# An attention and feed-forward kernel: all attention products in plain float32, eight first-stage weight chunks instead of six

## The chip, the cores and the metric

The kernel runs on one NeuronCore of a Trainium2 chip. The metric is the device time of one execution in microseconds (us). TensorE (PE) multiplies matrices; VectorE (DVE), ScalarE (ACT) and GpSimd (POOL) work on elements; SyncE (SP) issues the transfers between the large memory (HBM) and the on-chip memory. TensorE writes its results into eight PSUM banks of 128 x 512 float32 values, from which DVE or ACT copies them. Each engine runs its own list of instructions in order, and waits where an instruction needs another engine's result.

## The reference

```python
scores = q @ k.T / 8                       # B=4, H=8 heads, S=576 rows, D=64; causal mask
a = exp(scores - rowmax); a /= a.sum() + 1e-9
local = a @ v
q_p = where(q > 0, q, exp(q) - 1) + 1
mem_out = (q_p @ M_prev) / (q_p @ z_prev + 1e-6)
x = sigmoid(beta) * mem_out + (1 - sigmoid(beta)) * local   # -> (2304, 512)
h = x @ w_in                                # (2304, 2048)
g = (a0 + a1 h + a2 h^2 + a3 h^3) / (1 + |b0||h| + |b1| h^2 + 1e-6)
out = g @ w_out                             # (2304, 512)
```

The results are float32. `w_in` and `w_out` come as 64-bit floats, which the kernel turns into 32-bit ones itself.

## The kernel before

The attention is done in 16 units of work: 4 batches times 4 pairs of heads, `u` from 0 to 15. For a unit, `load` brings q, k and v of two heads, `prep` transposes q and k on TensorE (line L505) and makes the transposed, normalized `q_p` (tile `E`, then `f`). `scores` makes q.k for four 128-row tiles of each head (128, 256, 384 and 512 columns wide) and `tail` for the last 64 rows of both heads together. `prob` then makes the softmax of each: DVE adds the mask and takes the maximum (L706), ACT the exponential and its sum (L710), POOL or DVE the reciprocal's input (L718, L719), DVE the reciprocal (L721), and POOL, ACT or DVE scales the rows (L722 to L724). TensorE transposes the probabilities, they are copied to tiles `g0` and `g1`, and `av` multiplies them by v and adds the memory's part; its result, `x`, is written to the scratch tensor `xs` in HBM (`spill`).

TensorE is used in two number formats. Plain float32 (F32) is run as two passes over the columns for each product. The reduced format F32R is run as one, and keeps fewer digits; to get them back, an operand is split in two F32R parts, a rounded one (`hi`) and the rest (`lo`), and three products are made in place of one. `hi_lo` (L536 ff.) does the split out of PSUM: a copy on ACT or DVE (L541, L542), and a subtraction on DVE (L547), or on TensorE and ACT (L494 with `nid`, L545). Before the change all scores are made so: the split, transposed q and k (tile `tt`) are moved by transfers into the tiles `qk0` and `qk1`, in which the parts of one head stand under each other, so that two products per tile of rows do. For the products with v the first five units (`PLAIN`) use plain float32 (tiles `gp`, `vz`, `mz`, `fp`), the other eleven the split form (`g`, `vs`, `ms`, `f`, `fl`, and `s`, by which the two halves of a result are added).

The feed-forward part works on groups of 256 rows (9 of them) and on 16 chunks of 128 hidden columns. Its weights are converted to 32 bits and split (`weights`: four DVE instructions, two of POOL and one of ACT for each half of a chunk). The first `F0` = 6 chunks are kept from early on (tile `w`); the first stage runs all groups through them, from `xs`, and writes partial sums to `po`. The other ten (tiles `w2i`, `w2o`) use memory that the attention leaves at its end; the second stage runs all groups through them. For two chunks of a group TensorE makes 24 products of 256 columns (`bk<-xg,w`) and 12 of 512 (`bk<-w,gh` and `bk<-w,gl`), with a chain of element-wise work on DVE, ACT and POOL between them (`act_chain`).

The order of all instructions is set when the kernel is built: `Sched.place` takes, again and again, the operation that could start first by its own table of costs, ties broken by priority; buffers and PSUM banks are given out by `Tag.can` and `Tag.take`. On the chip the order of each engine's list is fixed, and only the waits decide when an instruction starts. The attention of unit `u` has priority 100 u and what follows, so it goes ahead of the feed-forward work, which fills what is free.

Of the kernel before, what the change touches and what calls it, by code (L numbers as in the profile page):

```python
# [25 lines left out]
SLOT = 150  # L26
# [64 lines left out]
class Tag:  # L91
# [8 lines left out]
    def can(self, seq):  # L100

        return len(self.free) > (0 if seq == self.head else 1)
# [15 lines left out]
class Sched:  # L118
# [64 lines left out]
    def place(self):  # L183
# [64 lines left out]
        while pend:  # L248
            best = None
            for o in pend:  # L250
                slot_t = 0.0
                ok = True
                for b in o.bufs:
                    if b.slot is None:
                        tg = b.tag
                        if not tg.can(b.seq) or b.kind and not b.kind.can(b.kseq):
                            ok = False
                            break
                        slot_t = max(slot_t, min(tg.free)[0] + SLOT)
# [57 lines left out]
def tile_attention_ffn(  # L317
# [105 lines left out]
    for n in ("qk0", "qk1"):
        for x in tags(atp, n, N[n], [128, 3, SM], F32R):
            for j in range(4):
                V.tensor_scalar(x[64:128, 2, 128 * j:128 * j + 128], idf[64:128, :], 0.0, None, op0=ALU.mult)

    tags(atp, "tt", N["tt"], [128, 4 * SM + 128], F32R)

    for x in tags(atp, "qd", N["qd"], [128, 2, 128], F32R):  # L430
        for i in range(2):
            r = slice(64 * i, 64 * i + 64)
            V.tensor_scalar(x[r, :, 64 - 64 * i:128 - 64 * i], idf[r, :].rearrange("p (a b) -> p a b", a=2), 0.0, None, op0=ALU.mult)
    tags(atp, "f", N["f"], [128, 2, S], F32R)
    tags(atp, "fl", N["fl"], [128, S], F32R)
    tags(atp, "vs", N["vs"], [128, 5, 4, 64], F32R)
    tags(atp, "ms", N["ms"], [128, KC, 4, 64], F32R)
    tags(atp, "mn", N["mn"], [128, KC, 2, 64])
# [6 lines left out]
    tags(atp, "g0", N["g0"], [128, 2, 384], F32R)  # L445
    tags(atp, "x", N["x"], [128, S])
    tags(atp, "s", N["s"], [128, 320], F32R)

    plx = ExitStack()
    if PLAIN:
        plp = plx.enter_context(tc.tile_pool(name="plp", bufs=1))
        tags(plp, "gp0", 1, [128, 2, 384])
        tags(plp, "gp1", 1, [128, 2, 4, 320])
        tags(plp, "fp", 1, [128, S])
        for n, shape in (("vz", [128, 5, 2, 128]), ("mz", [128, KC, 128])):
            for x in tags(plp, n, 1, shape):
                G.memset(x, 0.0)  # L460
    for i in range(2):
        sc.tag(f"g1{i}", 1).free = []
# [787 lines left out]
```

## Time and profile before

| | |
|---|---|
| median of 3 runs | 723.14 us (720.86 to 726.55) |
| profiled execution, first to last instruction | 722.8 us; no other time of it is given |
| attention (last write of `xs` issued) | 365 us |
| first stage's last product with `w_out` | about 456 us |
| TensorE's granted clock, mean | 0.974 of 2.4 GHz |

The page of the profile shows how long each engine was busy; TensorE's spans are modelled and overlap, so that a busy share near one is not yet its peak. How long a product really takes is read from the starts of instructions that follow each other without a gap.

### The profile page before, as it was taken

The numbers are of one execution on the slowest core, as the hardware profiler recorded it, in microseconds if no ns is written. First come the engines' busy times: TensorE is split into PE (matmuls) and PEld (weight loads), VectorE is DVE, ScalarE is ACT, GpSimd is POOL, SyncE is SP. The second block draws the span as 40 slices with busy tenths as digits, with TensorE's granted clock in tenths as the row PEclk, the third lists the DMA queues.
The fourth block names the chain that finished last, engine by engine and source line by source line (L and its number), as shares of the span: only waits on it lengthen the run. The fifth ranks groups of instructions, "written<-read, shape, count | busy, mean of one in ns | idle before, by whom it ended". The sixth has DMA issues, their size and how long they took to land.

```text
span 722.8 us, 12139 instructions
## 1 busy us (share of the span) xinstructions
PE 659.6 (91%) x3752; PEld 561.2 (78%) x3752; DVE 588.3 (81%) x1385; ACT 480.6 (66%) x1072; POOL 492.7 (68%) x599
## 2 busy tenths in 40 slices
PE   3879798799898999799999999886999999999997
PEld 2667576687777778688899998775998888788786
DVE  5787697799998999689877999989786776866775
ACT  2767576789888798769666766474575552851852
POOL 4476666678877679636568999769775663763763
PEclk9999989899999999899999999998999999999999
DMA  6877888685788774944267543721580103003001
GB/s 139 204 198 180 205 197 195 153 227 122 212 220 211 173 171 123 257 115 106 98 211 244 171 155 125 258 63 58 185 311 31 58 1 116 1 1 114 4 0 59
DMA packets 102577, 102.51 MB, mean 142 GB/s; under 512 B 67632, under 2 KB 80432, under 8 KB 100208
## 3 DMA queue, kind: packets, MB, share of 16 engines
q1 hardware_dynamic: 102512, 101.73, 50.4%
q8 instruction: 30, 0.49, 0.3%
q14 instruction: 35, 0.29, 0.1%
HBM read 52.27 MB, written 23.59 MB: 105 GB/s over the span
## 4 chain that ended last, share of the span: by engine, by line
PE 40%; DVE 22%; POOL 11%; ACT 9%; DMA 8%; issue 6%; SPq 3%; POOLq 0%; ACTq 0%; DVEq 0%
PE bk L494 37%; POOL tw L521 4%; PE bk L505 4%; DVE bk L706 3%; SPq L487 3%; DVE tb L1026 2%; DVE g L547 2%; DVE gh L527 1%; POOL tw L1021 1%; DVE bk L527 1%; ACT g L541 1%; DVE bk L1028 1%; DVE gl L1041 1%; ACT Ps L710 1%; DMA xf<-xs 1%
## 5 line engine op out<-in xcount | busy, mean ns | idle before, releaser
L494 PE MATMUL bk<-w2o,gh 128*128 128x512 f32 x360 | 111.1, 390 | 0.9 <-DVE gh L527 0.9
L521 POOL TENSOR_TENSOR tw<-tw,gh 128x512 f32<-128x512 f32 x60 | 77.8, 1301 | 33.2 <-DVE gh L527 33.0
L1021 POOL TENSOR_SCALAR tw<-ta,cb 128x512 f32<-128x512 f32 x71 | 57.4, 808 | 62.8 <-ACT ta L1017 62.4
L521 POOL TENSOR_TENSOR tw<-tw,ta 128x512 f32<-128x512 f32 x72 | 94.2, 1309 | 3.8
L1017 ACT ACTIVATE ta<-bk 128x512 f32<-128x512 f32 x72 | 42.8, 595 | 71.8 <-PE bk L494 53.6
L494 PE MATMUL bk<-w,w2i 128*128 128x512 f32 x360 | 84.9, 390 | 0.0
L494 PE MATMUL bk<-xg,w 128*128 128x256 f32 x648 | 83.5, 284 | 0.0
L494 PEld LDWEIGHTS bk<-xg,w 128*128 128x128 f32 x648 | 80.5, 191 | 2.8 <-ACT x L898 0.8
L706 DVE CUSTOM_DVE_ANT_0 bk<-bk,mk 128x512 f32<-128x512 f32 (+3 forms) x144 | 72.4, 519 | 11.7 <-PE bk L494 11.0
L494 PEld LDWEIGHTS bk<-w,w2i 128*128 128x128 f32 x360 | 67.3, 188 | 14.6 <-DVE gl L1041 0.5
L494 PE MATMUL bk<-w2o,gl 128*128 128x512 f32 x180 | 70.8, 393 | 8.6 <-DVE gl L1041 8.6
L1025 ACT ACTIVATE ta<-tw,lnb 128x512 f32<-128x512 f32 x72 | 52.0, 723 | 39.7 <-POOL tw L521 39.3
L494 PEld LDWEIGHTS bk<-w2o,gh 128*128 128x128 f32 x360 | 66.9, 188 | 14.6 <-DVE gh L527 1.3
L494 PE MATMUL bk<-qk 128*128 128x256 f32 (+3 forms) x256 | 67.4, 364 | 7.7 <-DMA qk<-tt 4.9
L527 DVE SCALAR_TENSOR_TENSOR bk<-bk,ca,tw 128x512 f32<-128x512 f32 x72 | 54.2, 753 | 21.9 <-POOL tw L521 21.6
L494 PE MATMUL bk<-w,gh 128*128 128x512 f32 x216 | 69.7, 404 | 0.0
L718 POOL TENSOR_SCALAR st<-st,g 128x1 f32<-128x1 f32 x88 | 26.5, 301 | 56.5 <-ACT Ps L710 47.1
L1026 DVE TENSOR_TENSOR tb<-bk,tb 128x512 f32<-128x512 f32 x72 | 49.3, 685 | 15.8 <-ACT tb L1018 12.6
L1028 DVE SCALAR_TENSOR_TENSOR bk<-tb,ca,bk 128x512 f32<-128x512 f32 x72 | 54.0, 750 | 9.1 <-ACT ta L1017 8.3
L527 DVE SCALAR_TENSOR_TENSOR gh<-bk,ca,ta 128x512 fp32r<-128x512 f32 x72 | 53.5, 743 | 8.1 <-PE bk L494 4.3
L547 DVE TENSOR_TENSOR g<-bk,g 128x512 fp32r<-128x512 f32 (+2 forms) x88 | 49.6, 567 | 8.7 <-ACT g L541 7.6
L710 ACT ACTIVATE Ps<-bk,st 128x128 f32<-128x128 f32 (+1 forms) x96 | 46.0, 482 | 11.5 <-DVE st L721 5.5
(151 smaller groups left out, 1702.0 us busy)
## 6 DMA issues: line engine op xcount, KB each, us to landing
qk<-tt SPq DMA_DIRECT2D x32, 384.0 KB, 4.7
xh<-xg SPq DMA_DIRECT2D x9, 1024.0 KB, 4.9
qk<-tt SPq DMA_DIRECT2D x32, 256.0 KB, 4.0
xf<-in_moe_w_in_dram SPq DMA_DIRECT2D x16, 512.0 KB, 4.7
xf<-in_moe_w_out_dram SPq DMA_DIRECT2D x16, 512.0 KB, 4.6
w<-xh SPq DMA_DIRECT2D x6, 1024.0 KB, 9.1
xs<-x SPq DMA_DIRECT2D x16, 288.0 KB, 2.3
xf<-xs SPq DMA_DIRECT2D x9, 512.0 KB, 5.8
```

The lines of the kernel that those rows point to most:

```text
L494: T.matmul(o, lhsT=l, rhs=r, start=s0, stop=s1, skip_group_check=more)
L505: T.matmul(o, lhsT=i, rhs=idn, start=x == 0, stop=True, is_transpose=True, skip_group_check=x > 0)
L521: opts = {"pool": ("pool", c_pool2(n), lambda: G.tensor_tensor(**kw()), "t"), "dve": ("dve", c_dve(n), lambda: V.tensor_tensor(**kw()), "2")}
L527: return dve(c_dve(n) + 61 * ap, lambda: V.scalar_tensor_tensor(out=out(), in0=in0(), scalar=scalar() if callable(scalar) else scalar, in1 ...
L547: dve(c_dve(n), lambda: V.tensor_tensor(out=lo(), in0=src(), in1=rb(hi()), op=ALU.subtract), [rsrc] + whi, wlo, pri)
L706: V.tensor_tensor_reduce(out=s, in0=s, in1=m, scale=-0.125, scalar=st.t[:, 0:1] if x else 3.0e38, op0=ALU.add, op1=ALU.min, accum_out=st.t ...
L710: act(c_act(w, ap=2), lambda bk=bk, w=w, x=x, c0=c0: A.activation(P.t[:, c0:c0 + w], bk.t[:, 0:w], AF.Exp, bias=st.t[:, mx:mx + 1], scale= ...
L1017: act(c_act(N), lambda: A.activation(a_(), h(), AF.Abs), [(hb, None)], [(ta, None)], p)
L1021: sc.op([("pool", c_pool(N, 2), lambda: G.tensor_scalar(w_(), a_(), cb[:, 1:2], cb[:, 0:1], op0=ALU.mult, op1=ALU.add), "s"), ("act", c_ac ...
L1025: act(c_act(N, False, 1), lambda: A.activation(a_(), w_(), AF.Ln, scale=2.0 ** -63, bias=lnb[:, 0:1]), [(tw, None)], [(ta, None)], p)
L1026: dve(c_dve(N), lambda: V.tensor_tensor(out=b_(), in0=h(), in1=b_(), op=ALU.mult), [(hb, None)], [(tb, None)], p)
L1028: dve(c_dve(N) + 61, lambda: V.scalar_tensor_tensor(out=h(), in0=b_(), scalar=ca[:, 1:2], in1=h(), op0=ALU.add, op1=ALU.mult), [(tb, None) ...
```

## The change

Every product of the attention is made in plain float32. `hi_lo`, the split tiles, the transfers `qk<-tt` and `f<-fl`, and the sum of halves (`s`, `fold`) are gone; a transposed q and k lie in one tile, `kt`, as they come out of PSUM, head 0 in partitions 0 to 63 and head 1 in 64 to 127. `scores` makes both heads' products one after the other, each on its own 64 partitions (64 rows of TensorE's array) and into its own bank. `av` makes one result for both heads: head 0 goes to partitions 0 to 63 of the bank, head 1 to 64 to 127, each with v as 64 columns of weights. Most attention tiles have two buffers instead of one (`nq`, `nk`, `kt`, `qd`, `g1`, `x`, ...), and `Tag.can` is asked for all of an operation's buffers at once. `FIRST` is 8 instead of 6, so the first stage has eight chunks and the second eight.

```diff
-FIRST = 6
-PLAIN = 5
+FIRST = 8
...
-N = {'tt': 1, 'f': 2, 'vs': 2, 'ms': 1, 'mn': 1, 'zb': 1, 'E': 1, 'den': 1, 'P': 4, 'Ps': 3, 'st': 8, 'g0': 2, 'x': 1, 's': 2, 'ta': 3, 'tb': 3, 'tw': 3, 'gh': 3, 'gl': 3, 'xf': 2, 'xg': 1, 'qk0': 1, 'qk1': 1, 'nq': 1, 'nk': 1, 'nv': 1, 'qd': 1, 'fl': 1, 'xf2': 2, 'pi': 2, 'wa2': 2}
+N = {'nq': 2, 'nk': 2, 'nv': 2, 'vt': 2, 'qd': 2, 'mz': 2, 'kt': 2, 'f': 2, 'zb': 1, 'E': 1, 'den': 2, 'P': 4, 'Ps': 6, 'st': 12, 'g0': 2, 'g1': 2, 'x': 2, 'ta': 3, 'tb': 3, 'tw': 3, 'gh': 3, 'gl': 3, 'xf': 2, 'xg': 1, 'xf2': 2, 'pi': 2, 'wa2': 2}
...
-    def can(self, seq):
-
-        return len(self.free) > (0 if seq == self.head else 1)
+    def can(self, seqs):
+
+        return len(self.free) >= len(seqs) + (0 if self.head in seqs else 1)
...
     def prep(u, p):
...
-        hi_lo(lambda: tl.t[:, 0:64], lambda: t.t[:, KT:KT + 64], lambda: t.t[:, KT + 64:KT + 128], 64,
-              (tl, None), (t, ("t", 0)), (t, ("t", 1)), p)
+        copy(64, lambda: kt.t[:, SM:S], lambda: tl.t[:, 0:64], [(tl, None)], [(kt, "t")], p)
...
-            hi, lo = (2, 3) if vi == 0 else (1, 0)
-            hi_lo(lambda bk=bk: bk.t, lambda hi=hi: t.t[:, SM * hi:SM * hi + SM], lambda lo=lo: t.t[:, SM * lo:SM * lo + SM], 512,
-                  (bk, None), (t, hi), (t, lo), p, "kq"[vi] in RES)
...
-            dma(lambda o=o, r=r: (rb(o.t[0:64].rearrange("p a b -> p (a b)")), rb(t.t[r, SM:KT])),
-                [(t, x) for x in (1, 2, 3)], [(o, 0)], p + 0.1 * i, 64 * SM * 12, late=1800.0)
-            dma(lambda o=o, r=r: (rb(o.t[64:128, 0:2]), rb(t.t[r, 0:KT].rearrange("p (a b) -> p a b", a=4)[:, 0:3:2])),
-                [(t, x) for x in (0, 2)], [(o, 1)], p + 0.1 * i, 64 * SM * 8, late=1800.0)
...
+            copy(SM, lambda c0=c0: kt.t[:, c0:c0 + SM], lambda bk=bk: bk.t, [(bk, None)], [(kt, n)], p)
...
-        hi_lo(lambda: bk.t, lambda: F.t[:, 0, 0:SM], lambda: lo()[:, 0:SM], SM, (bk, None), (F, (0, "m")), (L, (1, "m")), p, "f" in RES)
...
-            hs, ls = [(F, (0, x)) for x in "mt"], [(L, (1, x)) for x in "mt"]
-            dma(lambda: (rb(F.t[r1, 1]), rb(F.t[r1, 0])), hs, [(F, (2, 0))], p, 64 * S * 4)
-            dma(lambda: (rb(F.t[r0, 1]), rb(L.t[r1])), ls, [(F, (2, 1))], p, 64 * S * 4)
-            dma(lambda: (rb(F.t[r1, 0]), rb(L.t[r0])), ls, hs, p, 64 * S * 4)
...
+        copy(SM, lambda: F.t[:, 0:SM], lambda: bk.t, [(bk, None)], [(F, "m")], p)
...
-    def scores(u, i, t, p):
+    def scores(u, t, p):
+        bb, c = divmod(u, KC)
+        kt = ST[u]["kt"]
+        n = 128 * (t + 1)
+        bk = [bank(), bank()]
+        q0 = S + 128 * t
+
+        def f():
+            return [(bk[i].t[:, 0:n], kt.t[64 * i:64 * i + 64, q0:q0 + 128], kt.t[64 * i:64 * i + 64, 0:n], True, True) for i in range(2)]
+        P = [probs(n) for _ in range(2)]
+        mm(f, 1.5 * c_mm4(n) + 100, [(kt, "k"), (kt, "q")], [(x, None) for x in bk], p, take=P[0] + P[1])
+        return [prob(P[i], [(bk[i], n, mk[:, 512 - 128 * t:640], 0)], g1[:, 2 * c + i:2 * c + i + 1], n, p + 0.5 * i) for i in range(2)]
+
...
-            x = d["qk"][i].t
-            return [(x[:, 0, qs], x[:, 1 + b, 0:n]) for b in range(2)]
-        m, src = (3, d["t"]) if d["direct"] else (2, d["qk"][i])
-        P = probs(n)
-        mm(lambda: [(bk.t[:, 0:n], a, b, x == 0, x == m - 1) for x, (a, b) in enumerate(f())], (6 if d["direct"] else 2) * c_mm(n),
-           [(src, None)], [(bk, None)], p, take=P)
-        return prob(P, [(bk, n, mk[:, 512 - 128 * t:640], 0)], g1[:, 2 * c + i:2 * c + i + 1], n, p)
...
-        hi_lo(lambda: pt.t[:, 0:384], lambda: g.t[:, 0, :], lambda: g.t[:, 1, :], 384, (pt, None), (g, 0), (g, 1), p + 1, "1" in RES)
...
+            copy(384, lambda i=i: g.t[:, i], lambda pt=pt: pt.t[:, 0:384], [(pt, None)], [(g, i)], p + 1)
...
-    def av(u, i, ch, p):
...
+    def av(u, ch, p):
 
         d = ST[u]
         q0, n = (0, 256) if ch == 0 else (256, 320)
...
+        nv, vt, F, g, mz = d["nv"], d["vt"], d["f"], d["g1" if ch else "g0"], MZ[bb]
+        blk = [0, 0, 0, 128] if ch else [0, 128]
+
+        def f():
+            L = [(o.t[:, 0:n], mz.t[:, c], F.t[:, q0:q0 + n])]
+            if ch:
+                L.append((o.t[:, 256:n], vt.t, g.t[:, 0, 3, 192:256]))
+            for j, o0 in enumerate(blk):
                 for h in range(2):
...
-                    lv = vs.t[:, j, 2 * i:2 * i + 2].rearrange("p a b -> p (a b)")
-                    if ch == 0:
-                        rh = g.t[:, hl, 256 * j:256 * j + n - o0]
-                    else:
-
-                        c0 = (192, 512, 832, 0, 1152)[j]
-                        rh = g.t[:, hl, i].rearrange("p j q -> p (j q)")[:, c0:c0 + n - o0]
...
-        else:
-            act(c_act(n), lambda: A.copy(out=s.t[r, 0:n], in_=o.t[r2, 0:n]), [(o, None)], [(s, None)], p)
-            dve(c_dve(n), lambda: V.tensor_tensor(out=x.t[r, w], in0=o.t[r, 0:n], in1=rb(s.t[r, 0:n]), op=ALU.add),
-                [(o, None), (s, None)], [(x, (i, ch))], p)
+                    c0 = (192, 512, 832, 0)[j] if ch else 256 * j
+                    x = g.t[:, h].rearrange("p j q -> p (j q)") if ch else g.t[:, h]
+                    L.append((o.t[64 * h:64 * h + 64, o0:n], nv.t[:, j, h], x[:, c0:c0 + n - o0]))
+            return [(a_, l, r, x == 0, x == len(L) - 1) for x, (a_, l, r) in enumerate(L)]
+        mm(f, c_mm4(n) + sum(c_mm4(n - o0) for o0 in blk) + 0.5 * c_mm4(n) + (c_mm4(64) if ch else 0) + 100,
+           [(g, None), (nv, None), (vt, None), (mz, None), (F, None)], [(o, None)], p, more=True)
+        x = d["x"] = d.get("x") or sc.buf("x")
+        copy(n, lambda: x.t[:, q0:q0 + n], lambda: o.t[:, 0:n], [(o, None)], [(x, ch)], p)
...
-        for i in range(2):
-            tiles01(u, i, base + 10 + pr["head"] * i)
-            av(u, i, 0, base + pr["av0"] + pr["head"] * i)
+        tiles01(u, base + 10)
+        av(u, 0, base + pr["av0"])
         if u + 1 < U:
```

The built order shows three places. The first is TensorE's list at the scores of the first unit. Rows read: line, operation, result<-operands, shape of the result, and a count of equal rows; `bk` is a PSUM bank, `idf` the identity of a transposition, `qk` and `kt` hold q and k. Before:

```order
L494 MATMUL bk3_122<-tt0_143,qd0_144 128x64 x3
L494 MATMUL bk4_123<-tt0_143,qd0_144 128x512 x3
L494 MATMUL bk5_124<-qk00_133 128x128 x2
L505 MATMUL bk6_125<-idf_76,E0_155 128x64
L505 MATMUL bk7_126<-idf_76,E0_155 128x128 x4
L494 MATMUL bk0_119<-qk00_133 128x256 x2
L505 MATMUL bk1_120<-idf_76,P0_157 64x128
L505 MATMUL bk2_121<-idf_76,P0_157 128x128 x4
L494 MATMUL bk3_122<-qk10_138 128x128 x2
```

After:

```order
L465 MATMUL bk3_114<-kt0_141,qd0_133 128x64
L465 MATMUL bk4_115<-kt0_141,qd0_133 128x512
L465 MATMUL bk5_116<-kt0_141 128x128
L465 MATMUL bk6_117<-kt0_141 128x128
L465 MATMUL bk7_118<-kt0_141 128x256
L465 MATMUL bk0_111<-kt0_141 128x256
L465 MATMUL bk1_112<-kt0_141 128x384
L465 MATMUL bk2_113<-kt0_141 128x384
L465 MATMUL bk5_116<-kt0_141 128x512
L465 MATMUL bk6_117<-kt0_141 128x512
```

A head's two F32R products of a tile now are one F32 product of each head, the heads alternating between two banks, and the four tiles' scores stand directly behind each other.

The second place is TensorE's list at the last product of the attention (`f`,`ms` or `mz` is the memory's part; `g1` with `vs` or `nv` are the probabilities and v; `xg`,`w1` and `w1`,`gh`/`gl` are the first stage). Before:

```order
L494 MATMUL bk6_125<-xg0_205,w1_187 128x256 x12
L494 MATMUL bk4_123<-f0_147,ms0_152 128x320
L494 MATMUL bk4_123<-g1_1286,vs0_150 128x320 x3
L494 MATMUL bk4_123<-g1_1286,vs0_150 128x192
L494 MATMUL bk4_123<-g1_1286,vs0_150 128x64
L494 MATMUL bk4_123<-g1_1286,vs0_150 128x320 x3
L494 MATMUL bk4_123<-g1_1286,vs0_150 128x192
L494 MATMUL bk3_122<-xg0_205,w1_187 128x256 x24
L494 MATMUL bk1_120<-xg0_205,w1_187 128x256 x24
L494 MATMUL bk5_124<-w1_187,gh0_197 128x512 x2
```

After:

```order
L465 MATMUL bk1_112<-xg0_195,w1_177 128x256 x12
L465 MATMUL bk0_111<-f1_144,mz1_138 128x320
L465 MATMUL bk0_111<-g11_174,vt1_130 128x64
L465 MATMUL bk0_111<-g11_174,nv1_128 64x320 x6
L465 MATMUL bk0_111<-g11_174,nv1_128 64x192 x2
L465 MATMUL bk1_112<-xg0_195,w1_177 128x256 x12
L465 MATMUL bk7_118<-w1_177,gh1_188 128x512 x2
L465 MATMUL bk7_118<-w1_177,gl1_191 128x512
L465 MATMUL bk4_115<-w1_177,gh1_188 128x512 x2
```

A result of one head with full-width products has become one of both heads, whose 64-column products alternate between the heads (x6 is three of each). Ahead of this place stand 312 products `xg,w1` and 108 `w1,gh`/`gl` before, 252 and 48 after, of 648 and 324 before and 864 and 432 after; with the second stage there are 1008 of 256 columns and 1224 of 512 in all before, 1152 and 1152 after.

The third place is where the first product of the feed-forward part stands. Before:

```order
L494 MATMUL bk3_122<-g1_1286,vs0_150 128x64
L494 MATMUL bk3_122<-g1_1286,vs0_150 128x320 x3
L494 MATMUL bk3_122<-g1_1286,vs0_150 128x192
L505 MATMUL bk2_121<-idf_76,nk0_129 128x64
L505 MATMUL bk2_121<-idf_76,nq0_127 128x64
L505 MATMUL bk4_123<-idf_76,nq0_127 128x128 x4
L494 MATMUL bk7_126<-xg0_205,w1_187 128x256 x12
L505 MATMUL bk5_124<-idf_76,Ps1_162 128x128
L505 MATMUL bk5_124<-idf_76,Ps2_163 128x128 x2
L505 MATMUL bk0_119<-idf_76,P2_159 64x128
```

After:

```order
L465 MATMUL bk7_118<-g01_172,nv1_128 64x128 x2
L465 MATMUL bk1_112<-kt1_142 128x512
L465 MATMUL bk6_117<-kt1_142 128x512
L465 MATMUL bk3_114<-kt0_141 128x128
L465 MATMUL bk5_116<-kt0_141 128x128
L465 MATMUL bk2_113<-kt0_141,qd0_133 128x64
L465 MATMUL bk0_111<-xg0_195,w1_177 128x256 x12
L476 MATMUL bk7_118<-idf_76,Ps4_157 128x128 x3
L465 MATMUL bk0_111<-xg0_195,w1_177 128x256 x12
L476 MATMUL bk4_115<-idf_76,Ps5_158 128x128 x3
```

It stood behind the sixth unit's last product with v, and now stands behind the ninth unit's (nine products of `mz`,`f` with 320 columns precede it). Transpositions are 640 in both kernels.

## Rows read from the trace of the kernel before

**Rows 1.** The page's first part: engine, busy us, share of the span, xinstructions

```profile
PE 659.6 (91%) x3752; PEld 561.2 (78%) x3752; DVE 588.3 (81%) x1385; ACT 480.6 (66%) x1072; POOL 492.7 (68%) x599
```

**Rows 2.** Stretches: us, then each engine's busy us (instructions), granted clock, DMA share, GB/s

```profile
0.00:147.00 147.00, 114.55 (x594) 91.94 (x595) 111.39 (x381) 95.89 (x271) 89.55 (x146) 0.93 0.77 183
147.00:365.00 218.00, 203.84 (x1360) 175.64 (x1361) 198.32 (x593) 178.54 (x479) 154.82 (x227) 0.98 0.65 168
365.00:456.00 91.00, 91.00 (x567) 82.43 (x567) 81.28 (x122) 61.80 (x100) 78.53 (x74) 1.00 0.53 177
456.00:723.00 267.00, 250.22 (x1236) 211.16 (x1235) 197.36 (x292) 144.35 (x224) 169.75 (x155) 0.98 0.24 85
```

**Rows 3.** Single tiles: durations, then first and last start (den, xs, first-stage products)

```profile
L657 DVE TENSOR_REDUCE den<-nk x16: 799/810/820, 12.9 to 333.1; 128x10 f32<-128x640 f32 x16
...
L487 SPq DMA_DIRECT2D xs<-x x16: 320/344/728, 43.7 to 365.2; - x16
...
L494 PE MATMUL bk<-xg,w x648: 274/283/388, 147.3 to 436.4; 128*128 128x256 f32 x162
...
L494 PE MATMUL bk<-w,gh x216: 387/389/628, 175.6 to 455.4; 128*128 128x512 f32 x108
```

**Rows 4.** TensorE in order of time, 76.8 to 83 us: start, us, instructions

```profile
76.76 0.70 PE L494 MATMUL bk<-fp,mz 128*128 128x320 f32 x2
77.30 4.21 PE L494 MATMUL bk<-gp,vz 128*128 128x320 f32 x18
81.34 0.50 PE L505 MATMUL bk<-idf,Ps 128*128 128x128 f32 x3
...
82.47 0.71 PE L505 MATMUL bk<-idf,P 128*64 128x128 f32 x5
82.93 0.70 PE L494 MATMUL bk<-qk 128*128 128x128 f32 x4
```

**Rows 5.** The same view, 242.8 to 261.5 us

```profile
242.81 0.39 PE L494 MATMUL bk<-w,gh 128*128 128x512 f32 x1
243.04 0.40 PE L494 MATMUL bk<-w,gl 128*128 128x512 f32 x1
...
246.10 0.40 PE L494 MATMUL bk<-w,gl 128*128 128x512 f32 x1
246.43 0.27 PE L505 MATMUL bk<-idf,E 64*128 64x64 f32 x1
246.63 0.73 PE L494 MATMUL bk<-w,gh 128*128 128x512 f32 x2
...
259.82 1.62 PE L494 MATMUL bk<-xg,w 128*128 128x256 f32 x12
261.27 0.49 PE L505 MATMUL bk<-idf,Ps 128*128 128x128 f32 x3
```

**Rows 6.** Groups by line and shape: count, busy us, mean ns, idle before

```profile
L547 DVE TENSOR_TENSOR g<-bk,g 128x384 fp32r<-128x384 f32 x44 | 24.1, 550 | 4.2 <-ACT g L541 3.6
L547 DVE TENSOR_TENSOR g<-bk,g 128x512 fp32r<-128x512 f32 x33 | 22.6, 684 | 4.0 <-ACT g L541 3.8
...
L902 DVE TENSOR_TENSOR x<-bk,s 64x320 f32<-64x320 f32 x22 | 10.7, 485 | 1.7 <-ACT s L901 1.1
...
L988 DVE TENSOR_SCALAR bk<-ta 128x512 int32<-128x512 int32 x12 | 8.2, 685 | 0.0
...
L545 ACT CAST tt<-bk 128x512 fp32r<-128x512 f32 x26 | 14.8, 600 | 0.2
...
L901 ACT CAST s<-bk 64x320 fp32r<-64x320 f32 x22 | 9.2, 420 | 5.0 <-PE bk L494 4.2
...
L521 POOL TENSOR_TENSOR vs<-nv,vs 128x640 fp32r<-128x640 f32 x11 | 17.6, 1599 | 0.2
```

**Rows 7.** The chain that ended last, 291 to 305 us: start, length, what

```profile
291.71 6.70 DMA f<-f
298.43 6.27 DMA f<-fl
```

More of the change, by code (lines that the diff above doesn't have):

```diff
@@ L252, in place @@
                 ok = True
+                need, lim = {}, {}
                 for b in o.bufs:
                     if b.slot is None:
[L255 to L259, printed above, removed]
+                        need.setdefault(b.tag, []).append(b.seq)
+                        if b.kind:
+                            lim.setdefault(b.kind, []).append(b.kseq)
                     elif b.t0 > slot_t:
                         slot_t = b.t0
+                for tg, seqs in need.items():
+                    if not tg.can(seqs):
+                        ok = False
+                        break
+                    slot_t = max(slot_t, sorted(tg.free)[len(seqs) - 1][0] + SLOT)
+                ok = ok and all(tg.can(seqs) for tg, seqs in lim.items())
                 if not ok:
@@ L418, in tile_attention_ffn @@
         sc.tag(n, lim)
-    for n in "qkv":
+    for n in "qk":
         for x in tags(atp, "n" + n, N["n" + n], [128, 5, 2, 64]):
             G.memset(x[:, 4], 0.0)
[L423 to L438, printed above, removed]
+    tags(atp, "nv", N["nv"], [128, 4, 2, 64])
+    for n, shape in (("vt", [128, 128]), ("qd", [128, 128]), ("mz", [128, KC, 128])):
+        for x in tags(atp, n, N[n], shape):
+            G.memset(x, 0.0)
+    tags(atp, "kt", N["kt"], [128, S + SM])
+    tags(atp, "f", N["f"], [128, S])
     tags(atp, "zb", N["zb"], [128, DM])
@@ L444, in tile_attention_ffn @@
     tags(atp, "st", N["st"], [128, 6])
-    tags(atp, "g0", N["g0"], [128, 2, 384], F32R)
+    tags(atp, "g0", N["g0"], [128, 2, 384])
+    tags(atp, "g1", N["g1"], [128, 2, 4, 320])
     tags(atp, "x", N["x"], [128, S])
[L447 to L462, printed above, removed]
     w1 = w1p.tile([128, F0, 2, 2, DM], F32R, name="w1")
@@ new lines, in tiles01 @@
+    def tiles01(u, p):
+        d = ST[u]
+        P = [scores(u, t, p + t) for t in range(2)]
+        g = d["g0"] = sc.buf("g0")
+        for i in range(2):
+            pt = bank()
+            src = ((0, 0), (1, 0), (1, 128))
+            tr(lambda i=i, pt=pt: [(b4(pt)[:, x, :], P[t][i].t[:, c0:c0 + 128], idf) for x, (t, c0) in enumerate(src)], 3 * 109,
+               [(P[0][i], None), (P[1][i], None)], [(pt, None)], p + 1, [g])
+            copy(384, lambda i=i: g.t[:, i], lambda pt=pt: pt.t[:, 0:384], [(pt, None)], [(g, i)], p + 1)
@@ L767, in tile23 @@
[L767 to L787 removed]
+        P = scores(u, t, p)
@@ new lines, in tile23 @@
+        if "g1" not in d:
+            d["g1"] = sc.buf("g1")
+        g = d["g1"]
+        for i in range(2):
+            pt = bank()
+            tr(lambda i=i, pt=pt: [(b4(pt)[:, x, :], P[i].t[:, 128 * j:128 * j + 128], idf) for x, j in enumerate((3, 0, 1, 2)[3 - t:])],
+               109 * (t + 1), [(P[i], None)], [(pt, None)], p, [g])
+            copy(n, lambda i=i: g.t[:, i, 0:3, 192:320] if t == 2 else g.t[:, i, :, 0:128], lambda pt=pt: b4(pt)[:, 0:t + 1, :],
+                 [(pt, None)], [(g, (i, t))], p)
@@ L831, in av @@
-    def av(u, i, ch, p):
+        copy(512, lambda: g.t[:, :, :, 128:192].rearrange("p a j q -> p j a q"),
+             lambda: pt.t.rearrange("p (j a q) -> p j a q", j=4, a=2), [(pt, None)], [(g, "t")], p)
+        for i in range(2):
+            r = slice(64 * i, 64 * i + 64)
+            copy(64, lambda r=r: g.t[r, 0, 3, 192:256], lambda r=r: p2.t[0:64, r], [(p2, None)], [(g, ("u", i))], p)
+    def av(u, ch, p):
         d = ST[u]
         q0, n = (0, 256) if ch == 0 else (256, 320)
-        if d["plain"] and i == 0:
-            return
```

254 lines of the change are left out of this document (32 added, 222 removed).

## The prediction

> **What bounds the kernel now.** I read first the page's busy shares, then the stretches, then TensorE in order of time. The busy shares [rows 1] put PE first at 91%, but its spans overlap, so the reader should price products by starts that follow each other: 0.23 us for an F32R product of 512 columns (243.04 less 242.81), 0.121 for one of 256 (261.27 less 259.82, twelve of them) [rows 5]. With the counts of the built order the feed-forward part is 1008 x 0.121 + 1224 x 0.23 = 404 us of TensorE, most of the 723.
>
> The stretches [rows 2] show three regimes. Until 147 us no feed-forward product runs [rows 3], and no engine is full: DVE 111 of 147 us (0.76), ACT 96, POOL 90. From 147 to 365 attention and first stage run together, and DVE is the fullest: 198 of 218 (0.91). After 365, when the last `xs` is written [rows 3], only feed-forward work is left: 696 products of 256 columns and 1116 of 512, or 84 + 257 = 341 us of TensorE in 358. So the time is the attention's end, 365, plus 341, plus 17 of gaps; the attention stretch is limited by DVE and by waits, the rest by TensorE. A unit takes (333.1 - 12.9) / 15 = 21.3 us [rows 3]. Waits of the split form stand on the chain too: the transfers `f<-f` and `f<-fl` hold it for 13 us from 291.7 on [rows 7].
>
> **The change, part by part.** The sum is made against the profiled execution, 722.8 us, 0.3 under the median of the runs.
>
> *DVE, ACT, POOL: less.* The subtractions of L547 and the sums of L902 go. The two largest groups are 24.1 and 22.6 us, L902 is 10.7 [rows 6]; with the smaller groups of L547 it is 85 us. Two more weight chunks are prepared before the attention's end: four halves of four instructions of about 0.68 us (L988's mean, [rows 6]), 11 us. Fewer feed-forward chains fall in the stretch (below). DVE's 310 us until 365 [rows 2] become some 225. ACT loses L545, 14.8, and the copies to `s`, 9.2 and a like amount [rows 6], and keeps one copy for every split: 274 becomes some 235. POOL loses the split of v, 17.6 and its smaller half [rows 6]: 244 becomes some 215.
>
> *Transfers: gone.* `qk<-tt` and `f<-fl` are on no list any more. I give that no term of its own: it is part of why units should follow each other more closely.
>
> *TensorE: more in the attention.* Plain float32 takes 4.04 us for 18 instructions, nine products of 2368 columns in all (81.34 less 77.30) [rows 4]: 1.70 us per 1000 columns, both passes included, where F32R takes 0.45. A unit's scores are 1280 columns for each head; in 16 units 40,960 columns, 69.6 us if no two run at once, 34.8 if the two heads run beside each other. I assume that a head's second pass follows its first on the same 64 rows; then, in the order head 0 first, head 0 second, head 1 first, head 1 second, only the middle two can overlap: three quarters, 52.2 us. No row shows products on different parts of the array at once, so this is my choice between the ends; the order of the passes is the reason. Entering the 64-row form costs: 246.10 to 246.43 is 0.33 us where 0.23 is usual, and leaving it 0.20 (to 246.63) where 64 columns take some 0.06 [rows 5]. That is 0.24 for each of 64 pairs, 15 us. Tails: 576 x 16 columns, 15.7. Products with v: the memory's and the tail's full-width ones 17.4; the heads' 3072 x 16 columns 83.6 one by one, 41.8 in pairs, and since heads alternate, half plus one lone pass for each result (0.49 a unit): 49.6. Transpositions: 640 x 0.11 (five in 0.46, [rows 4]) = 70.4. Sum: 52.2 + 15 + 15.7 + 17.4 + 49.6 + 70.4 = **220 us**, 13.8 a unit. The ends are 272 (17.0 a unit; no overlap) and 196 (12.2; full).
>
> Entering the 64-column form shows no price: the transposition of 64 columns and four others fill 0.46 us, as five usual ones would [rows 4]. The Trainium skill says, in TensorEngine Tiling (Array Packing), Key Properties, that a change of tiling mode drains TensorE; the trace agrees for the row form and not for the column form. By that rule the 32 results with v would pay the 0.24 as well, 8 us, and the sum below would be 704.
>
> *Attention's end.* Ahead of its last product stand 252 x 0.121 + 48 x 0.23 = 41.5 us of feed-forward work (62 before), all of it behind the ninth unit. Nine units alone: PE 124 us, and DVE, ACT and POOL near it (9/16 of their loads is about 120 to 130). With two buffers a unit can run into the next, but no engine is far ahead of the others and nothing fills the waits. I take a share of 0.80, a little over the 0.76 of the first stretch [rows 2]: 155 us. Seven units with filling: 97 + 41.5 = 138, at the 0.91 of the second stretch: 152. A start of 10 us (the first `den` is at 12.9, [rows 3]). End: 317, where 365 stood.
>
> *After it.* 900 products of 256 and 1104 of 512 are left: 109 + 254 = 363 us, 22 more than before, because the attention's stretch holds less of them. Gaps 17, as before: fewer weight chunks remain (eight, not ten), but POOL's 78.5 of 91 us from 365 to 456 [rows 2] shows how little room that stretch has.
>
> Sum: 317 + 363 + 17 = **697 us**, 3.6% under the median. What is late next is TensorE itself.
>
> **Rivals.**
> *No overlap on the array.* If head 1 starts only when head 0 is done, the attention is 272 us on TensorE. Nine units are 153 and seven 160; TensorE then leads clearly, so shares of 0.88 and 0.93: 174 + 172 + 10 = 356, and 356 + 380 = **736 us**, slower. For it: no row shows an overlap. Against it: the two heads use other rows, other columns and other banks. It decides where less than about a third of the pairs' time is saved. This is also the case in which the change doesn't do what it says.
>
> *Full overlap, or waits that vanish.* With 196 us TensorE's 237 in the stretch equal ACT's 235; at 0.82 that is 289 + 10, and the time **679 us**. The same comes out if the first nine units reach 0.91. For it: every single-buffered tile of the chain is doubled. The Trainium skill's page TensorEngine Tiling (Array Packing), in Key Properties, says that tiles operate independently and in parallel, and by that rule both heads' passes would run side by side; nothing here shows it.
>
> *Units still follow each other one by one.* The softmax's chain crosses four engines for each tile, `E` and `zb` keep one buffer, and two banks must be free at once for the scores. If a unit stays at 20 us as in the first stretch, nine take 180: 180 + 152 + 10 + 380 = **722 us**, no change. Against it: the transfer and the split in the chain are gone, and DVE's load falls by a quarter.
>
> **How the numbers follow.** What a measurement here can tell from no change is 1%, 716 to 730 us. The forecast, 697, has a chance of 0.45 (685 to 712); full overlap or vanished waits 0.22 (664 to 684); units one by one 0.15; no overlap 0.13; 0.05 is left for something unseen, mostly slow. Faster: 0.44 of the forecast, 0.22, and 0.05 of the third rival, 0.71. Same: 0.01, 0.06 of the third and 0.04 of the no-overlap case, 0.11. Slower: the rest, 0.18. The range from 664 to 736 leaves out half of the no-overlap case and the unseen ones, and some of the lowest.
>
> **What would show it.** In the changed kernel's trace: the last write of `xs` near 317 (356 without overlap, 342 one by one); the distance of `den` reductions near 17 us in the first nine units; the starts of a pair's four passes, of which the middle two should coincide; the 64-column products of a result in about half of 1.70 us per 1000 columns; DVE's busy time under 235 until the attention's end; and after it 363 us of products with under 20 of gaps. Wrong it would be if first-stage work after the attention waits for POOL or the late weights (gaps of 40 and more), or if TensorE, with nothing to fill the first nine units, is granted the lower clock for much of them (0.93 in the first stretch, [rows 2]).

## The result: 661 us where 697 were forecast

The changed kernel takes 661.44 us (median of 4 runs, 659.89 to 663.24), the kernel before 723.94 beside it (720.86 to 726.55): a ratio of 0.9137, 95% interval 0.9107 to 0.9167. That is 8.6% faster; the forecast was 3.6%, and its range, 664 to 736, ended above the result. The profiled execution has a span of 658.1 us, against which the parts are counted below.

The profile after, the page's first part, answers to [rows 1]:

```profile
PE 630.4 (96%) x3744; PEld 496.7 (75%) x3744; DVE 530.2 (81%) x1229; ACT 444.0 (67%) x987; POOL 452.1 (69%) x553
```

TensorE is busy for 96% of a shorter span, DVE for as large a share as before with 58 us less. The stretches, cut at the same events as [rows 2] (first feed-forward product, attention's end, end of the first stage); columns as there:

```profile
0.00:165.00 165.00, 143.76 (x878) 88.83 (x880) 140.84 (x489) 132.91 (x392) 123.58 (x204) 0.98 0.58 155
165.00:294.00 129.00, 127.34 (x868) 93.32 (x865) 99.81 (x315) 100.22 (x267) 80.38 (x123) 1.00 0.26 75
294.00:464.00 170.00, 170.00 (x1074) 154.64 (x1074) 150.15 (x224) 107.62 (x172) 130.92 (x122) 1.00 0.41 139
464.00:658.00 194.00, 189.27 (x932) 159.92 (x930) 139.38 (x203) 103.25 (x160) 117.23 (x106) 1.00 0.23 87
```

The reader should see the second column against the first: TensorE has 143.76 of 165 us, then 127.34 of 129, then all of 170. Single tiles, as in [rows 3]:

```profile
L579 DVE TENSOR_REDUCE den<-nk x16: 794/812/822, 14.6 to 246.5; 128x10 f32<-128x640 f32 x16
...
L458 SPq DMA_DIRECT2D xs<-x x16: 320/339/1082, 31.5 to 294.3; - x16
...
L465 PE MATMUL bk<-xg,w x864: 277/283/685, 165.5 to 442.4; 128*128 128x256 f32 x173
...
L465 PE MATMUL bk<-w,gh x288: 389/389/791, 220.0 to 460.0; 128*128 128x512 f32 x144
```

A unit takes (246.5 - 14.6) / 15 = 15.5 us, where it took 21.3. The attention ends at 294 and not at the forecast 317, and what follows takes 658.1 - 294.3 = 364 us and not 380. TensorE in order of time, a piece of one unit (start, us, instructions):

```profile
97.35 0.60 PE L465 MATMUL bk<-f,mz 128*128 128x256 f32 x2
97.88 0.87 PE L465 MATMUL bk<-g,nv 128*64 128x256 f32 x8
98.68 0.49 PE L465 MATMUL bk<-kt 64*128 64x128 f32 x4
...
100.76 0.70 PE L465 MATMUL bk<-kt 64*128 64x256 f32 x4
101.50 0.83 PE L476 MATMUL bk<-idf,E 128*128 128x128 f32 x5
...
105.39 0.92 PE L465 MATMUL bk<-kt 64*128 64x384 f32 x4
106.23 0.81 PE L465 MATMUL bk<-f,mz 128*128 128x320 f32 x2
106.88 0.33 PE L465 MATMUL bk<-g,vt 128*128 128x64 f32 x2
107.14 2.16 PE L465 MATMUL bk<-g,nv 128*64 128x320 f32 x16
109.23 0.55 PE L476 MATMUL bk<-idf,Ps 128*128 128x128 f32 x3
```

The sixteen passes from 107.14 on are four for each of three blocks of 320 columns and one of 192: 2304 columns of products in two passes, 3.9 us at the 1.70 us per 1000 columns of [rows 4]. They take 2.09 (to 109.23). Both heads run side by side in all of their passes here. The starts of single passes in the trace show it too: the two first passes of this result start at 107.136 and 107.143, the two second ones at 107.456 and 107.463. The scores do the same (98.679 and 98.686, then 98.892 and 98.899). So it is in all 32 results with v, and in 54 of the 64 pairs of scores; in the other ten some of head 1's passes start 0.09 to 0.43 us after head 0's.

### The profile page after: what moved, and what is told of

It is laid out like the page before. It is cut to its first block, busy times and chain, and to the rows that moved or that the text cites. A ratio compares the mean times of both kernels' runs of the same rounds, so it can differ in the third digit from the quotient of the medians.

```text
span 658.1 us, 11480 instructions
## 1 busy us (share of the span) xinstructions
PE 630.4 (96%) x3744; PEld 496.7 (75%) x3744; DVE 530.2 (81%) x1229; ACT 444.0 (67%) x987; POOL 452.1 (69%) x553
## 4 chain that ended last, share of the span: by engine, by line
PE 74%; DVE 9%; ACT 7%; POOL 5%; issue 2%; DMA 2%; SPq 1%; POOLq 0%; ACTq 0%; DVEq 0%
PE bk L465 68%; PE bk L476 6%; DVE bk L605 2%; ACT Ps L609 1%; ACT g L470 1%; ACT P L609 1%; POOL Ps L621 1%; DMA xf<-in_moe_w_in_dram 1%; SPq L458 1%; POOL nk L492 1%; DVE E L498 1%; POOL st L617 1%; DVE tb L819 1%; POOL E L492 1%; DVE bk L783 1%
## 5 line engine op out<-in xcount | busy, mean ns | idle before, releaser
L465 PE MATMUL bk<-xg,w 128*128 128x256 f32 x864 | 111.0, 285 | 0.0
L465 PEld LDWEIGHTS bk<-xg,w 128*128 128x128 f32 x864 | 106.8, 191 | 2.7 <-issue 1.5
L465 PE MATMUL bk<-w,gh 128*128 128x512 f32 x288 | 90.5, 395 | 0.0
L465 PE MATMUL bk<-w2o,gh 128*128 128x512 f32 x288 | 88.7, 390 | 0.0
L605 DVE CUSTOM_DVE_ANT_0 bk<-bk,mk 128x384 f32<-128x384 f32 (+3 forms) x144 | 71.5, 520 | 8.2 <-PE bk L465 8.0
L465 PE MATMUL bk<-w,w2i 128*128 128x512 f32 x288 | 67.7, 390 | 0.0
L470 ACT COPY g<-bk 128x384 f32<-128x384 f32 (+2 forms) x128 | 58.2, 496 | 7.4 <-PE bk L476 6.4
L465 PEld LDWEIGHTS bk<-w,w2i 128*128 128x128 f32 x288 | 53.9, 188 | 11.7 <-DVE gl L834 0.5
L811 ACT ACTIVATE tb<-bk,ca 128x512 f32<-128x512 f32 x59 | 45.6, 773 | 24.1 <-PE bk L465 23.9
L465 PEld LDWEIGHTS bk<-w,gh 128*128 128x128 f32 x288 | 52.2, 188 | 11.4 <-issue 1.1
L465 PE MATMUL bk<-w,gl 128*128 128x512 f32 x144 | 56.1, 389 | 0.0
## 6 DMA issues: line engine op xcount, KB each, us to landing
w<-xh SPq DMA_DIRECT2D x6, 1024.0 KB, 11.9
```

What stands on the lines that cost most here:

```text
L465: T.matmul(o, lhsT=l, rhs=r, start=s0, stop=s1, skip_group_check=more)
L470: sc.op([("act", c_act(n), lambda: A.copy(out=out(), in_=in_())), ("dve", c_dve(n), lambda: V.tensor_copy(out(), in_()))], reads, writes, pri)
L605: V.tensor_tensor_reduce(out=s, in0=s, in1=m, scale=-0.125, scalar=st.t[:, 0:1] if x else 3.0e38, op0=ALU.add, op1=ALU.min, accum_out=st.t ...
L811: sc.op([("act", c_act(N, ap=2), lambda: A.activation(b_(), h(), AF.Identity, scale=ca[:, 3:4], bias=ca[:, 2:3])), ("dve", c_dve(N) + 61, ...
```

## The experiments

All are edits of the changed kernel, each run with the kernel before on the same chip; the ratio is to that one, with its 95% interval. The last column sets the median against the changed kernel's 661.44. The chips differ: the kernel before had medians of 722.8 to 725.6 us on them, so 3 us in the last column say little, and the intervals decide.

| run | us | ratio (interval) | us more |
|---|---|---|---|
| six first weights kept | 678.45 | 0.9379 (0.9336 to 0.9421) | 17.0 |
| v products by head | 676.14 | 0.9338 (0.9291 to 0.9385) | 14.7 |
| scores on the same rows | 684.65 | 0.9458 (0.9404 to 0.9511) | 23.2 |
| both of these | 703.44 | 0.9714 (0.9670 to 0.9759) | 42.0 |
| no overlap at all | 722.44 | 0.9973 (0.9943 to 1.0004) | 61.0 |
| single buffers | 674.07 | 0.9309 (0.9260 to 0.9358) | 12.6 |
| a VectorE pass after each copy | 710.42 | 0.9796 (0.9746 to 0.9847) | 49.0 |
| v products by twos | 660.72 | 0.9145 (0.9108 to 0.9182) | -0.7 |
| pairs priced, weights later | 655.05 | 0.9069 (0.9037 to 0.9101) | -6.4 |
| the same, more buffers | 658.37 | 0.9126 (0.9087 to 0.9165) | -3.1 |
| six kept, short late weights | 663.85 | 0.9157 (0.9095 to 0.9219) | 2.4 |
| eight kept, short late weights | 660.05 | 0.9112 (0.9059 to 0.9164) | -1.4 |

### Is it the overlap?

The products with v in another order:

```
-            for j, o0 in enumerate(blk):
-                for h in range(2):
+            for h in range(2):
+                for j, o0 in enumerate(blk):
```

> The heads' products with v in another order, all blocks of head 0 and then all of head 1, same products, same plan. They can then not run beside each other except where one head ends and the next begins: 41.8 us more on TensorE. Theory 1 (the pairs run side by side, and TensorE bounds the whole attention): nearly all of it is paid, 695 to 705. Rival 1 (TensorE bounds only the last seven units, the first nine have room): 7/16 of it, near 680. Rival 2 (no overlap was there, or waits decide): 661.

676.14 us, which looks like the first rival but isn't, since TensorE did not get 41.8 us more. Its order of time, one result of two blocks and one of four:

```profile
104.79 0.88 PE L465 MATMUL bk<-g,nv 128*64 128x256 f32 x8
...
114.05 3.29 PE L465 MATMUL bk<-g,nv 128*64 128x320 f32 x16
```

The results of two blocks still overlap fully (0.88 us, 0.87 before the edit); those of four take 3.29 where they took 2.16. That is 1.13 x 16 = 18 us, of which 14.7 were paid. In the single starts head 0's first pass of the second result is at 114.046, and head 1's first, the ninth in the list, at 115.180, beside head 0's fifth at 115.174. So a product of the other column half started ahead of four passes that stand before it, and not ahead of more. That became theory 4, and this edit tests it:

```
-            for j, o0 in enumerate(blk):
-                for h in range(2):
+            for j, h in [(2 * a + b, h) for a in range(len(blk) // 2) for h in range(2) for b in range(2)]:
+                    o0 = blk[j]
```

> The heads' products with v in yet another order: two blocks of head 0, two of head 1, and so on, same products, same plan. Theory 4 (the products of one column half start ahead of up to four passes of the other half that stand before them, as the order by head showed: its results of two blocks overlapped fully, those of four blocks only from the fifth pass on): with four passes of a head in a row every pair still overlaps, TensorE's time for them stays at 46 to 49 us and the time is 659 to 664. Rival (only neighbours overlap, and every change of head costs): half of the pairs lost, some 21 us on TensorE, time 672 to 680.

660.72 us, and the same result in the trace:

```profile
108.11 2.21 PE L465 MATMUL bk<-g,nv 128*64 128x320 f32 x16
```

2.21 us beside 2.16: with four passes of one head in a row hardly anything is lost, as theory 4 has it. So TensorE does not start its products strictly in the order of its list, as the text ahead of the prediction says of every engine. The scores, next:

```
-kt.t[64 * i:64 * i + 64, q0:q0 + 128], kt.t[64 * i:64 * i + 64, 0:n]
+kt.t[0:64, q0:q0 + 128], kt.t[0:64, 0:n]
```

> Both heads' scores are computed from head 0's q and k, so that a pair uses the same 64 rows; the same number and shape of products, the same plan. Theory 1 (all four passes of a pair had overlapped two by two, TensorE bounds): 34.8 us more on TensorE, nearly all paid, 690 to 697, and the starts of the four passes follow one another by a pass each. As predicted (only the middle two overlapped): 17 us more. Rival (first nine units have room): 676. No overlap before: 661.

684.65 us. The groups of the four shapes of scores, in this run (columns: count, busy us, mean ns, idle before), give 90.3 us of TensorE's time:

```profile
L465 PE MATMUL bk<-kt 64*128 64x512 f32 x64 | 32.8, 634 | 0.0
...
L465 PE MATMUL bk<-kt 64*128 64x384 f32 x64 | 26.0, 528 | 0.0
L465 PE MATMUL bk<-kt 64*128 64x256 f32 x64 | 19.4, 426 | 0.0
...
L465 PE MATMUL bk<-kt 64*128 64x128 f32 x64 | 12.1, 307 | 1.3 <-ACT P L609 1.0 <-ACT g L470 0.3
```

The same four groups are 17.8 + 16.2 + 11.9 + 9.5 = 55.4 in the changed kernel, so 34.9 were added, where full overlap gives 34.8 and the forecast's three quarters 17. Of the 34.9, 23.2 were paid. The time lies between theory 1's 690 and the rival's 676: full overlap, but the attention has some room. Both edits together:

> Both edits together (both heads' scores from head 0's rows, products with v by head): 77 us more on TensorE. Theory 1: 733 to 740, which is the no-overlap rival's 736 of the prediction. Rival (room in the first nine units): 695 to 705. If the sum is less than that of the two alone, another engine covers part.

703.44 us for 53 us of products: 42 paid, near the sum of the two alone (38). It lies in the rival's range only because the order by head broke less than half of the overlap of the products with v (18 of 41.8 us). To break all of them, both heads' products with v went into the same columns:

```
-o.t[64 * h:64 * h + 64, o0:n]
+o.t[0:64, o0:n]
```

> Both heads' scores from head 0's rows, and both heads' products with v into the same 64 columns of the result (head 1's half of the result is left out): no pair can overlap, the same products and the same plan. TensorE has 34.8 + 41.8 = 77 us more in the attention. Theory 1 (TensorE bounds the attention, by the slope of the three runs before: 43 us of time for 53.5 of products): 294 + 62 = 356 for the attention's end, time 718 to 726. The prediction's no-overlap sum: 736. Rival (other engines cover more, the longer it is): near 705, as with the scores and the order by head alone.

722.44 us, inside theory 1's band. **Without the overlap the change is worth nothing**: the ratio to the kernel before is 0.9973, with 1 in its interval. One result with v, and the last write of `xs`:

```profile
108.05 4.09 PE L465 MATMUL bk<-g,nv 128*64 128x320 f32 x16
```

```profile
L458 SPq DMA_DIRECT2D xs<-x x16: 320/339/347, 38.8 to 355.7; - x16
```

The attention ends at 355.7, and 364 us follow, as in the changed kernel. Over the four runs TensorE's additions of 18, 35, 53 and 75 us (the last by the same groups, with 94.9 us of products with v beside 53.9) cost 15, 23, 42 and 61: two thirds to four fifths is paid.

### The eight kept chunks

```
-FIRST = 8
+FIRST = 6
```

> Six first weights kept, as before, all else as changed. Theory 1 (eight kept chunks took the 17 us of gaps after the attention away): gaps after the last write of xs return, about 17 us, and the time is near 678. Rival (attention with fewer splits and TensorE as its bound did all of it, the chunks only move products from one stage to the other): 661 within 7 us.

678.45 us, theory 1. The attention even ends a little earlier (last `xs` at 287.2), but 676.6 - 287.2 = 389 us follow. TensorE's waits from 360 to 520 us (us in total, times, longest), in the kernel before and in this run; the changed kernel has none there:

```profile
PE bk L494 <- DVE gl L1041: 6.2, 2, 4.2
PE bk L494 <- DMA xg<-xh: 2.6, 1, 2.6
```

```profile
PE bk L465 <- DVE gl L834: 6.1, 5, 3.5
PE bk L465 <- POOL w2i L492: 2.3, 2, 1.9
```

Most of the waiting, in both, is for `gl`, which VectorE writes in the activation's chain; a late weight itself (`w2i`) ends only 2.3 us of it in this run. TensorE in the middle of this run, with what its idle time waited for:

```profile
453.82 0.74 PE L465 MATMUL bk<-xg,w2i 128*128 128x256 f32 x4 [1.89 <-POOL w2i L492]
454.40 0.62 PE L465 MATMUL bk<-w2o,gh 128*128 128x512 f32 x2
458.51 0.80 PE L465 MATMUL bk<-w2o,gl 128*128 128x512 f32 x1 [3.49 <-DVE gl L834]
```

And its stretches from the attention's end (columns as above):

```profile
287.00:420.00 133.00, 130.85 (x829) 119.01 (x829) 122.93 (x180) 80.70 (x132) 102.54 (x97) 1.00 0.53 184
420.00:470.00 50.00, 42.23 (x238) 36.47 (x237) 44.43 (x67) 23.41 (x37) 37.06 (x36) 0.93 0.17 55
470.00:676.00 206.00, 198.80 (x927) 164.80 (x925) 146.20 (x212) 110.97 (x171) 121.00 (x109) 1.00 0.20 74
```

From 420 to 470 TensorE has 42 of 50 us and DVE 44; the last late weight is written at 465.4. Theory 6: ten late chunks have to be prepared while only 133 us of first stage are left, DVE (122.93 of 133) cannot, and TensorE waits. With eight kept there are eight late chunks and 170 us. To test it, two of the four VectorE instructions for each half of a late chunk were left out. The two that stay then write into the weight's own tile, no longer into a PSUM bank:

```
+late = f >= F0
-wp = sc.buf("bk", "w")
+wp = wu if late else sc.buf("bk", "w")
...
-dve(c_dve(512) + 60, lambda pi=pi, hi32=hi32: V.scalar_tensor_tensor(
+late or dve(c_dve(512) + 60, lambda pi=pi, hi32=hi32: V.scalar_tensor_tensor(
...
-dve(c_dve(512) + 60, lambda lo32=lo32, ui=ui, pi=pi: V.scalar_tensor_tensor(
+late or dve(c_dve(512) + 60, lambda lo32=lo32, ui=ui, pi=pi: V.scalar_tensor_tensor(
```

> Six first weights kept, and of the ten late chunks' weights the sign and the low bits are left out: two of four VectorE instructions for each of their twenty halves, some 25 us of VectorE less in the stretch after the attention. Theory 6 (with six kept chunks the ten late ones come too late, because VectorE cannot prepare them while the shorter rest of the first stage runs; that is what the eight kept chunks mend): the gaps before the last late weight, 13 us in all with six chunks kept, shrink to under 4, and the time is 662 to 669. Rival (the gaps come from the activation's chain or from reading xh back, not from late weights): 675 to 679.

> The same two VectorE instructions left out for the eight late chunks of the changed kernel, its control. Theory 6: no late weight holds TensorE there, nothing is gained: 658 to 663. Rival (VectorE's load after the attention costs time in the changed kernel too): 645 to 656.

663.85 and 660.05 us: 14.6 us gained with six kept, and with eight 1.4, which the intervals cover. The same middle stretch of the first of them:

```profile
420.00:470.00 50.00, 49.32 (x330) 45.27 (x329) 37.44 (x56) 33.34 (x52) 38.18 (x36) 1.00 0.43 169
```

TensorE is at 49.32 of 50, the last late weight is written at 437.3, not 465.4, and TensorE's waits after 365 us fall from 14.0 to 3.1 us. Theory 6 holds for the changed kernel with six kept: the preparation of the late weights on VectorE made the gaps. That the PSUM bank, which both runs leave free, did it instead is made unlikely by the control, which gains nothing by it. For the kernel before nothing of the kind was run; its waits, above, are alike.

### What made the units dense

One buffer for most tiles of the attention, and fewer of `Ps` and `st`:

```
-'nq': 2, 'nk': 2, 'nv': 2, 'vt': 2, 'qd': 2, 'mz': 2, 'kt': 2, 'f': 2, 'zb': 1, 'E': 1, 'den': 2, 'P': 4, 'Ps': 6, 'st': 12, 'g0': 2, 'g1': 2, 'x': 2
+'nq': 1, 'nk': 1, 'nv': 1, 'vt': 1, 'qd': 1, 'mz': 1, 'kt': 1, 'f': 1, 'zb': 1, 'E': 1, 'den': 1, 'P': 4, 'Ps': 4, 'st': 8, 'g0': 1, 'g1': 1, 'x': 1
```

> The changed kernel with one buffer each of nq, nk, nv, vt, qd, mz, kt, f, den, g0, g1 and x, four of Ps and eight of st. Theory 2 (double buffers let a unit run into the next, which is why TensorE's share came out at 0.87 and 0.99, not 0.80 and 0.91): the attention's end goes back to about 317 (0.80 and 0.91 of the same products), time 680 to 692. Rival (the shorter chain, without split and transfer, did it, so buffers add little): 661 to 668.

674.07 us, between the two ranges. In the profiled execution, the slowest of its four (677.3 us), the attention ends at 327.9, later than theory 2 has it, but the planner lets feed-forward products into the waits, so 349 us follow, not 364. The buffers are worth 13 us together. Then the work of the old split, put back on VectorE:

```
...
+        if more:
+            dve(c_dve1(n), lambda: V.tensor_scalar(out(), out(), 1.0, None, op0=ALU.mult), [], writes, pri, "1")
```

> A VectorE pass over each tile that a copy from PSUM has written (times 1, in place), where the old kernel had its split: some 16 more VectorE instructions in a unit, 65 to 75 us in all, in the chain and on the engine; TensorE's work stays. Theory 3 (VectorE's load and the longer chain held the old attention back): the first stretch, in which VectorE is at 0.85, grows by most of what is added, attention's end 330 to 350, time 695 to 715. Rival (TensorE alone decides now, VectorE has room): under 675.

The tile `x` is left out of it. 710.42 us, in theory 3's range, but its account of the attention misses: the last `xs` is written at 387.6, where it had 330 to 350, and the first feed-forward product starts at 181.4 instead of 165.5, so the first stretch grows by 16 us of the 64 that VectorE has more. The planner moved feed-forward products ahead of the attention's end, and 320 us follow, not 364. Its first 330 us:

```profile
0.00:170.00 170.00, 131.77 (x687) 79.91 (x687) 147.06 (x489) 111.60 (x324) 105.33 (x181) 0.87 0.46 122
170.00:330.00 160.00, 153.51 (x967) 111.04 (x966) 146.25 (x426) 117.42 (x310) 112.67 (x159) 0.96 0.32 94
```

VectorE's share hardly rises, from 0.85 to 147.06 / 170 = 0.87, while TensorE's falls from 0.87 to 0.78 with a granted clock of 0.87 in place of 0.98: with more waits, more of that stretch ran at the lower of its two levels, 1.2 GHz. 64 us more of VectorE cost 49, and TensorE's additions were paid at two thirds to four fifths: both bound the attention. The run does not tell VectorE's load from the chain's added length, nor how much of the loss the lower clock is.

### Better than both

The planner charges a pair one pass and a half; the pair takes one. Priced so, and with the weights prepared later:

```
-1.5 * c_mm4(n) + 100
+1.0 * c_mm4(n) + 250
...
-sum(c_mm4(n - o0) for o0 in blk) + 0.5 * c_mm4(n)
+sum(c_mm4(n - o0) for o0 in blk) + 250
...
-'w': 50.2
+'w': 70
```

> The planner charges a pair of products one pass for both heads, and 0.25 us for the changes of form, in place of one and a half; and the eight first weights are prepared with more distance (70 in place of 50.2), so that the first nine units have VectorE more to themselves. Theory 5 (VectorE, at 0.85, and TensorE, at 0.87, share the bound of the first stretch, and weights there come too early): attention's end some 15 to 20 us earlier, of which the feed-forward products that no longer stand ahead of it are given back; time 650 to 657. Rival (TensorE's 630 us of 658 leave nothing, or the later weights become a wait): 658 to 666.

655.05 us, in theory 5's range; the interval of its ratio lies below the changed kernel's, and below that of the order by twos on the same chip. Its last `xs` is written at 266.6, 28 us earlier where 15 to 20 were expected, and most of that is given back by the feed-forward products which no longer stand ahead of it:

```profile
0.00:165.00 165.00, 146.86 (x885) 90.58 (x885) 139.89 (x482) 133.18 (x404) 129.28 (x214) 0.99 0.56 148
165.00:280.00 115.00, 114.86 (x791) 83.86 (x790) 90.20 (x296) 90.18 (x251) 73.38 (x117) 1.00 0.32 97
```

TensorE has 146.86 of the first 165 us, 3 more than in the changed kernel, and 114.86 of the next 115. The two edits weren't run apart. With more buffers:

```
-'E': 1
+'E': 2
...
-'ps0': 5
+'ps0': 6
```

> As the run before, with a second buffer of E and six banks, not five, for the first units. Theory 5: the feature map of the next unit no longer waits for E, so a few us more than the run before: 646 to 655. Rival (TensorE is full, or banks taken by the attention keep the first stage out): 656 to 666.

658.37 us, a miss for theory 5 and in the rival's range: TensorE has 140.60 of the first 165 us there. The cause stays open.

## Why the prediction was wrong, by its steps

**The step that failed first** is "then, in the order head 0 first, head 0 second, head 1 first, head 1 second, only the middle two can overlap: three quarters", and the same with one lone pass for each result with v. In all results with v and in 54 of 64 pairs of scores the passes overlap two by two. The reason given, the order of the passes, was wrong: a pass of the other half does not wait for the neighbour's passes that stand before it, up to the four that the runs tried. With three quarters TensorE had 220 us in the attention, with all 196. The prediction had the price: its full-overlap rival ends the attention at 299, 18 us before the forecast's 317; without the overlap, as a run, the attention ends at 355.7 and the time is 722.44.

**The second** is "Gaps 17, as before". It saw that fewer weight chunks remain and set POOL's load in that stretch against it. What makes the gaps with six kept chunks is the preparation of late weights on VectorE, and the eight kept chunks took them away: 364 us follow the attention, not 380, and with six kept the time is 678.45, beside the rival's 679. That is 16 us. The rival with full overlap kept these 17 us of gaps; its own 299 and the 363 of products would have been 662, but no branch of the prediction, and so not its range, had both.

697 - 18 - 16 = 663; the remaining 5 us of the profiled execution (658.1) are the attention's end at 294, not 299.

**The sums inside fit better than their total.** Full overlap and 8 us for the column form (below) make 204 us of TensorE in the attention by the prediction's own prices. At its own shares that is 115 / 0.80 = 143 for nine units, and with 41.5 of feed-forward work 131 / 0.91 = 144 for seven: with the start of 10 the end is 297, and 294 was measured. So the shares held in sum, and the overlap was the step. The trace agrees with the 204 + 41.5: the single products at the usual distances are 221 us until then, and the changes of form some 23. The profile's busy time, 143.76 + 127.34 us, is more, since a product's modelled end reaches over a short wait behind it; 0.87 and 0.99 in the expectations above are shares of that time, and can't be set beside 0.80 and 0.91. The no-overlap rival's attention, 356, was measured as 355.7, in part by luck, as it had nothing for the column form; its 736 is too high by the gaps alone.

**The change of form.** The prediction let the 64-column form enter free, on the transposition in [rows 4]. That row misled: in the trace after, six of the sixteen transpositions of that shape follow on work of the usual form, and five of these start at the usual distance of about 0.11 us, as does what follows on them. The products with v do pay. From 97.35 to 97.88 two passes of `mz` take 0.53 us, where twice 0.218 is usual, and from 97.88 to 98.68 the result takes 0.80 for 0.65; the second result pays 0.15 and 0.13. That is about 0.26 for each of 32 results, 8 us, the amount that the rule gave. The Trainium skill's TensorEngine Tiling (Array Packing), Key Properties, says that a change of tiling mode drains TensorE and that tiles operate independently; the trace agrees in that such a change costs time, though not at the transposition, and that the halves run side by side. The row form cost 0.28 for the pair at 105.39: 0.09 on entry (from 104.87, 0.52 for 0.43), and 0.20 from its start to the next (0.85, for twice 0.327), a little over the 0.24 assumed. Twelve of the 64 pairs stand directly behind another pair and enter free.

**What held.** The split's work left DVE, ACT and POOL: 241, 233 and 204 us until the attention's end, against 225, 235 and 215; DVE is over the 235 given as a sign. The products left after the attention were 363 us by count, 364 follow, and TensorE is what is late next. The units did not follow one by one: the first nine come every 14.4 us (`den` from 14.6 to 129.9), where 17 was forecast.

## What to carry to other kernels

Where two products use different row or column halves of the array, count the time of one, also for float32 in two passes, and give the planner that price; but keep the other half's product within four passes of its own in the list, since behind eight it was late. When a change shortens a stage, ask what was prepared in its shadow: here the weights for the next stage, and two more chunks kept were worth a quarter of the whole gain. And let two terms that may miss in the same direction do so together in one rival: here full overlap and vanished gaps were each thought of, but the range had no case with both.

## What the runs showed that was not expected

- Where the heads alternate, the two halves' passes start 6 to 7 ns apart, for row halves and for column halves.
- A pass of one column half started ahead of four passes of the other that stand before it (2.21 us for a result in that order, 2.16 for alternate heads); with eight before it, it started beside the fifth (3.29 us).
- The change to a half form costs some 0.1 us on entry and 0.1 on leaving, and between the first and second passes another 0.05 for column halves and 0.1 for row halves, whatever the width: two passes of a pair of scores start 0.213 us apart at 128 columns, where 0.109 is usual, and 0.53 at 512 (110.03 to 110.57), where 0.43 is. A pair directly behind another pair of scores enters free.
- A transposition with 64 columns pays none of this; one on 64 rows does, 0.20 us to the next start where its 64 columns take some 0.06.
